# Trailing the second half of each output block by one more step, and spreading the second batch's filter products wider

## The chip, the cores and the metric

The kernel runs on one core of a Trainium2 chip. The metric is device time in microseconds (us) for one launch, and the time given for a kernel is the median of its runs. All profile times are us from the start of the profiled span, unless they are marked ns.

## The reference, cut to what matters

```python
# x: 8 batches x 3008 positions x 256 channels
X = np.fft.rfft(x, axis=1)
Y = X * (filt_r + 1j * filt_i)[None]          # one complex filter per frequency and channel
y = np.fft.irfft(Y, n=3008, axis=1)           # 24064 tokens x 256
h = y.reshape(24064, 256) @ w_in              # 256 -> 2048
g = h * sigmoid(beta * h)
out = g @ w_out                               # 2048 -> 256, float32
```

So there are two stages: a filter along the sequence, done batch by batch, and a two-layer network over all tokens.

## The kernel before

**The network.** The 24064 tokens are cut into 47 blocks of 512, and the hidden width of 2048 into 16 slices of 128. One *step* is one slice of one block, so there are 752 steps, and step s belongs to block s // 16. In a step TensorE makes the hidden slice `hps` (two matmuls of 512 columns), ScalarE applies the activation and writes `gT`, and some steps later TensorE takes `gT` as weights and adds the slice's part to the output sums `acc` (four matmuls of 256 columns, numbered tb 0 to 3, one for each 128 tokens of the block). Sums tb 0 and 1 share one PSUM bank (half 0 of a block), tb 2 and 3 another (half 1). The pool `opsum` has three banks and hands them out in turn: block i half 0, block i half 1, block i+1 half 0, and then block i+1 half 1 gets the bank of block i half 0 again. VectorE copies a finished bank to the SBUF tile `ost` (pool of two), and SyncE's queue stores `ost` to DRAM.

**The lag.** `lags[i]` says for each tb how many steps after its hidden slice the output matmul is issued. It is 2 for all four, except in the last block (2, 2, 4, 6). `gT` has seven buffers.

**The filter.** The Fourier transform of 3008 = 47 x 64 positions is done in four matmul stages, and for batches 1 to 7 these are strewn between the steps of the network: a dictionary `plan` lists, for each step, the helper calls that are issued after the step's hidden matmuls and before its output matmuls. In order, for a batch b:

- `load_x` (POOL's queue) brings x; `s1` (16 calls) makes the first transform into `a1`; `a2_load` turns `a1` by eight transposing DMAs in SyncE's queue.
- `s2` (12 calls) is the second transform and the filter product. TensorE makes two matmuls of 256 columns into a bank; VectorE makes three products of 512 elements a partition (`a_t`, and `b_t` in two halves); GpSimd adds them to `yh`.
- `s3` (12 calls, each a fixed number of steps after its `s2`) is the first inverse transform: two matmuls, and a copy into `z`. For batch 1 that copy is on ScalarE. After every third `s3` a DMA in SyncE's queue stores `z` to the scratch `d2`.
- `zz_load` brings `d2` back in four pieces (one for each two values of `jq`), again in SyncE's queue; the first waits until all of `d2` has landed.
- `s4` (16 calls) is the last transform. It writes `y`, which the network reads.

Batch 0 is done ahead of the steps, apart from the `f_late` and `z_late` calls in steps 1 to 26. `s1`, `s2`, `s3`, `s4` and `f_late` all draw from one pool of three PSUM banks, `fpsum`.

**Order.** The program is written in the order in which each engine runs it (a manual schedule). An engine works through its own list, and waits at an instruction until what it needs is there. So a call's step sets its place in every list: TensorE's, VectorE's, ScalarE's, GpSimd's and the queues of DMAs. A queue with nothing to wait for runs ahead of the step.

The main loop, for one step s: hidden matmuls, activation, the calls of `plan[s]`, then the output matmuls listed for s. With equal lags this list holds the four matmuls of slice s-2; after the last slice of a block both halves are copied out one after the other:

```python
    for h in range(2):
        evac(ost[:, 2 * h : 2 * h + 2, :], acc[i, h][:], False)
```

For batch 1 the filter products stand at steps 23 to 46, each `s3` five steps later (28 to 51), `zz_load` at step 54, `s4` at steps 66 to 78; the `s1` calls of batch 2 stand at steps 54 to 76, and the loads of batch 3's x at 62, 68, 88 and 92.

Of the kernel before, what the change touches and what calls it, by code (L numbers as in the profile page):

```python
# [10 lines left out]
P = 128  # L11
# [4 lines left out]
F32 = mybir.dt.float32  # L16
# [20 lines left out]
def kernel(  # L37
# [12 lines left out]
    B, S, D = x.shape  # L50
# [11 lines left out]
    NBLK = TOK // TB  # L62
# [43 lines left out]
    st = {}  # L106

    def evac(dst, src, on_act, scale=None):
        if on_act:
            nc.scalar.activation(dst, src, ACT.Copy, scale=1.0 if scale is None else scale)  # L110
        elif scale is None:
            nc.vector.tensor_copy(dst, src)  # L112
        else:
            nc.vector.tensor_scalar_mul(dst, src, scale)  # L114
# [440 lines left out]
    ostp = ctx.enter_context(tc.tile_pool(name="ostp", bufs=2, **tw))  # L555
# [116 lines left out]
    def at(s, fn, *a):  # L672
        plan.setdefault(int(s), []).append((fn, a))

    def s1_steps(b, units_, steps, act, on_act=()):
        assert len(steps) == len(units_)
        for i, s in zip(units_, steps):
            at(s, s1, b, i, i in on_act)

    def s23_steps(b, steps, lag, act):  # L680
        assert len(steps) == NU
        for i, s in enumerate(steps):
            at(s, s2, b, i)
            at(s + lag, s3, b, i, i % act == act - 1 if act else False)

    def s4_steps(b, steps, act):
        assert len(steps) == J // 4 * NDC
        for i, s in enumerate(steps):
            at(s, s4, b, i, i % act == act - 1 if act else False)

    for b in range(1, B):
        o = first_step[b - 1]
        if b == 1:
            at(1, z_late, 1, 0)
            at(2, z_late, 1, 1)
            s1_steps(1, range(16), [5 + (2 * i + 1) // 3 for i in range(16)], False, (1, 4, 7, 10, 13))
            for i, r in enumerate((3, 4, 5, 6)):
                at(r, f_late, 1, i // 2, i % 2)
            for g in range(NG):
                at(o + 17, a2_load, 1, g)  # L700
            for hh, z0, f0 in ((2, (4, 4), (16, 18, 19, 20)), (3, (5, 5), (21, 22, 24, 26))):
                for e in range(NDC):
                    at(z0[e], z_late, hh, e)
                for i, r in enumerate(f0):
                    at(r, f_late, hh, i // 2, i % 2)
            s23_steps(1, [o + r for r in (23, 25, 27, 29, 31, 34, 36, 38, 40, 42, 44, 46)], 5, 1)
            for h in range(J // JG):
                at(o + 54, zz_load, 1, h)
            s4_steps(1, [o + 66 + (i * 12) // 15 for i in range(16)], 2)
            at(0, scale_wout, 2 * WG)  # L710
            at(0, load_wout, 3 * WG)
            at(1, scale_wout, 3 * WG)
            if B > 2:
                for g in range(4):
                    at(o + 24 + 3 * g, load_x, 2, g)
                late = (54, 55, 56, 57, 58, 59, 60, 61, 66, 67, 68, 70, 72, 73, 74, 76)
                s1_steps(2, range(16), [o + r for r in late], False)
                for g in range(NG):
                    at(o + 80, a2_load, 2, g)
                if B > 3:  # L720
                    for g in range(4):
                        at(o + (62, 68, 88, 92)[g], load_x, 3, g)
            continue
        base = [o + 16 * n + s for n in range(4) for s in (4, 8, 12)]
        if b == 2:
            base[:6] = [o + r for r in (8, 12, 19, 22, 26, 29)]
        s23_steps(b, base, 6, False)
        for h in range(J // JG):
            at(o + 70, zz_load, b, h)
        s4_steps(b, [o + 80 + (i * 13) // 15 for i in range(16)], False)  # L730
        if b + 1 < B:
            early = [o + 16 * n + s for n in range(4) for s in (7, 13)]
            late = [o + s for s in (66, 67, 69, 70, 72, 73, 75, 76)]
            s1_steps(b + 1, range(16), early + late, False)
            for g in range(NG):
                at(o + 82, a2_load, b + 1, g)
            if b + 2 < B:
                for g in range(4):
                    at(o + (30, 62, 88, 92)[g], load_x, b + 2, g)

    blk = {}
    acc = {}
    lags = {i: (2, 2, 2, 2) for i in range(NBLK)}
    lags[NBLK - 1] = (2, 2, 4, 6)
    outs = {}
    for s in range(NSTEP):
        i, fb = divmod(s, NFB)
# [3 lines left out]
    def acc_of(i, tb):  # L751
        h = tb if i == NBLK - 1 and tb == 3 else tb // 2
        if (i, h) not in acc:
            acc[i, h] = opsum.tile([P, 2, D], F32, name="acc", tag="acc")
        return acc[i, h]

    def out_block(i):
        ost = ostp.tile([P, 4, D], F32, name="ost", tag="ost")
        rows = out[i * TB : (i + 1) * TB, :].rearrange("(c p) d -> p c d", p=P)
        for h in range(2):  # L760
            evac(ost[:, 2 * h : 2 * h + 2, :], acc[i, h][:], False)
        if i < HB:
            for h in range(2):
                off = (i * JG + 4 * h) * D
                dst = AP(out.tensor, out.offset + off, [[J * D, M], [D, 4], [1, D]])
                nc.sync.dma_start(dst, ost[h * M : (h + 1) * M, :, :])
            return
        nc.sync.dma_start(rows, ost[:])

    def out_last(i, tb, ost):  # L770
        rows = out[i * TB : (i + 1) * TB, :].rearrange("(c p) d -> p c d", p=P)
        if tb == 1:
            evac(ost[:, :2, :], acc[i, 0][:], True)
            nc.sync.dma_start(rows[:, :2, :], ost[:, :2, :])
        elif tb > 1:
            evac(ost[:, tb, :], acc_of(i, tb)[:, tb % 2, :], False)
            (nc.scalar if tb == 2 else nc.sync).dma_start(rows[:, tb, :], ost[:, tb, :])

    for s in range(NSTEP + 4):
        if s < NSTEP:  # L780
            i, fb = divmod(s, NFB)
            t0 = i * TB
            hps = hpsum.tile([P, TB], F32, name="hps", tag="hps")
            pos = t0
            while pos < t0 + TB:
                b, n0 = divmod(pos, S)
                ln = min(S - n0, t0 + TB - pos)
                for dc in range(NDC):
                    nc.tensor.matmul(  # L789
                        hps[:, pos - t0 : pos - t0 + ln],  # L790
                        lhsT=win_sb[:, dc, fb * P : (fb + 1) * P],
                        rhs=ys[b][:, dc, n0 : n0 + ln],
                        start=(dc == 0),
                        stop=(dc == NDC - 1),
                    )
                pos += ln
            gT = gpool.tile([P, TB], BF16, name="gT", tag="gT")
            nc.scalar.activation(gT[:], hps[:], ACT.Silu, scale=beta_sb[:, fb : fb + 1])  # L798
            blk[s] = gT
        for fn, a in plan.get(s, ()):  # L800
            fn(*a)
        last = NBLK - 1
        if s == NSTEP - 1:
            ost = ostp.tile([P, 4, D], F32, name="ost", tag="ost")
        for i, fb, tb in outs.get(s, ()):
            lone = i == last and tb > 1
            nc.tensor.matmul(  # L807
                acc_of(i, tb)[:, tb % 2, :],
                lhsT=blk[i * NFB + fb][:, tb * P : (tb + 1) * P],
                rhs=wout_sb[:, fb, :],  # L810
                start=(fb == 0 and (tb % 2 == 0 or lone)),
                stop=(fb == NFB - 1),
                skip_group_check=True,
            )
            if fb == NFB - 1:
                if i == last:
                    out_last(i, tb, ost)
                elif tb == 3:
                    out_block(i)
# [1 line left out]
_INS = ['x', 'filt_r', 'filt_i', 'moe_w_in', 'moe_w_out', 'moe_beta']  # L821
_OUTS = [((24064, 256), 'float32')]
# [25 lines left out]
```

## Time and profile before

| what | value |
|---|---|
| median of 3 runs | 774.1 us (773.82 to 774.34) |
| the profiled execution, its own time | 773.73 us |
| its span | 772.0 us |
| granted TensorE clock | 0.999 |
| TensorE matmul busy | 757.2 us, 98% |
| TensorE weight load busy | 547.9 us, 71% |
| ScalarE busy | 552.2 us, 72% |
| VectorE busy | 431.6 us, 56% |
| GpSimd busy | 152.9 us, 20% |

The profile belongs to one execution, whose time is 1.7 us above its span and 0.4 us below the median of the runs. In the profile PE is the matmul half of TensorE and PEld its weight load, DVE is VectorE, ACT ScalarE, POOL GpSimd, and SPq or POOLq the queue of DMA issues of that engine. L807 is line 807, the output matmul; L789 the hidden matmul; L798 the activation; L591 `s2`; L605, L606 and L609 its products; L610 the sum; L623 `s3`; L630 the store to `d2`; L635 `zz_load`; L645 `s4`; L564 `s1`; L580 `a2_load`; L112 VectorE's copies; L171 the loads of x. A matmul's duration includes its way through the array, so consecutive durations overlap; the distance between two starts tells how long one holds the engine.

### The profile page before, as it was taken

Reading aid. Unit: us, or ns where it says so; the run is one execution under the profiler, and the core shown is the slowest. Engines: PE = TensorE matmul, PEld = TensorE weight load, DVE = VectorE, ACT = ScalarE, POOL = GpSimd, SP = SyncE. Lnnn points to the kernel's source line nnn. Section 1 sums busy time; section 2 is a strip of 40 time slices with the busy share of each in tenths; the row PEclk is TensorE's granted clock in tenths of the full one; section 3 lists DMA queues with packets and bytes.
Section 4 is the critical chain, followed back from the end, with each engine's and each line's share of the span. In section 5 each row is a group of like instructions: output and inputs, shape, how many; then the busy total and the mean of one; then the engine's idle time right before and its main releaser. Section 6 shows DMA issues by size and latency. Waiting matters only on the chain.

```text
span 772.0 us, 15747 instructions
## 1 busy us (share of the span) xinstructions
PE 757.2 (98%) x6255; PEld 547.9 (71%) x6351; DVE 431.6 (56%) x712; ACT 552.2 (72%) x813; POOL 152.9 (20%) x155
## 2 busy tenths in 40 slices
PE   8899999999999999999999999999999999999997
PEld 5676777777777777867778777776777766676665
DVE  8869654765556655666456664566745665321001
ACT  7777877776677766777667776677766777777776
POOL 7805301222012220122101322022200222000000
PEclk9999999999999999999999999999999999999999
DMA  9998476334813258141672317621146111500101
GB/s 197 238 174 167 118 165 116 73 107 96 195 39 100 65 128 173 35 110 49 160 142 70 76 49 184 129 64 48 49 130 138 49 49 49 157 28 29 56 28 54
DMA packets 108348, 78.78 MB, mean 102 GB/s; under 512 B 53916, under 2 KB 101276, under 8 KB 108276
## 3 DMA queue, kind: packets, MB, share of 16 engines
q1 hardware_dynamic: 101876, 64.24, 32.1%
q0 software_dynamic: 4192, 13.40, 10.2%
q8 instruction: 49, 0.80, 0.4%
q10 hardware_dynamic: 2208, 0.14, 0.2%
q14 instruction: 23, 0.19, 0.1%
HBM read 43.46 MB, written 35.65 MB: 102 GB/s over the span
## 4 chain that ended last, share of the span: by engine, by line
PE 93%; DVE 3%; ACT 2%; issue 1%; POOL 0%; DVEq 0%; POOLq 0%
PE acc L807 43%; PE hps L789 39%; PE ps L645 3%; PE ps L564 3%; PE ps L623 2%; PE ps L591 2%; DVE a_t L605 1%; DVE b_t L606 1%; DVE b_t L609 0%; DVE ost L112 0%; ACT y L110 0%; ACT aT L110 0%; ACT t L110 0%; DVE pq_t L430 0%; PE sps L444 0%
## 5 line engine op out<-in xcount | busy, mean ns | idle before, releaser
L798 ACT ACTIVATE gT<-hps,beta_sb 128x512 bf16<-128x512 f32 x752 | 516.4, 687 | 207.4 <-PE hps L789 180.2
L807 PE MATMUL acc<-wout_sb,gT 128*128 128x256 bf16 x3008 | 453.3, 272 | 2.4
L789 PE MATMUL hps<-y,win_sb 128*128 128x512 bf16 (+7 forms) x1634 | 427.6, 350 | 0.2
L807 PEld LDWEIGHTS <-gT 128*128 128x128 bf16 x3008 | 280.8, 98 | 101.9 <-issue 1.2
L610 POOL TENSOR_TENSOR yh<-a_t,b_t 128x512 bf16<-128x512 f32 x84 | 106.6, 1269 | 419.2 <-DVE b_t L609 418.4
L789 PEld LDWEIGHTS <-win_sb 128*128 128x128 bf16 x1728 | 164.7, 98 | 24.5 <-DVE y L114 0.3
L112 DVE COPY ost<-acc 128x512 f32<-128x512 f32 (+1 forms) x94 | 60.0, 680 | 139.7 <-PE acc L807 139.7
L114 DVE TENSOR_SCALAR y<-ps 128x376 bf16<-128x376 f32 (+2 forms) x128 | 63.3, 510 | 61.9 <-PE ps L645 59.1
L605 DVE TENSOR_TENSOR a_t<-ps,fr_sb 128x512 f32<-128x512 f32 x84 | 58.1, 692 | 68.1 <-PE ps L591 67.5
L112 DVE CAST a<-ps 128x384 bf16<-128x384 f32 x107 | 59.1, 557 | 58.3 <-PE ps L564 47.8
L606 DVE SCALAR_TENSOR_TENSOR b_t<-ps,fi_sb 64x512 f32<-64x512 f32 x84 | 58.2, 693 | 1.1
L609 DVE TENSOR_TENSOR b_t<-ps,fi_sb 64x512 f32<-64x512 f32 x84 | 57.4, 684 | 1.1
L112 DVE CAST z<-ps 128x512 bf16<-128x512 f32 x72 | 49.4, 686 | 1.9 <-PE ps L623 1.0
L645 PEld LDWEIGHTS <-zz 96*128 96x128 bf16 x448 | 29.7, 97 | 22.9
L564 PEld LDWEIGHTS <-xg 94*128 94x128 bf16 x448 | 30.4, 97 | 19.9
L564 PE MATMUL ps<-t,xg 94*128 94x96 bf16 x448 | 36.7, 205 | 0.8
L645 PE MATMUL ps<-t,zz 96*128 96x94 bf16 x448 | 34.7, 205 | 1.1
L591 PE MATMUL ps<-a,t 128*128 128x256 bf16 x168 | 32.1, 273 | 0.6 <-DVE b_t L609 0.3
L623 PE MATMUL ps<-yh,t 128*128 128x256 bf16 x168 | 32.1, 272 | 0.5 <-DVE b_t L609 0.2
L623 PEld LDWEIGHTS <-t 128*128 128x128 bf16 x168 | 16.1, 98 | 18.1 <-issue 1.5
L591 PEld LDWEIGHTS <-t 128*128 128x128 bf16 x168 | 16.0, 98 | 16.6 <-DVE b_t L609 0.5
L171 POOL DMA_DIRECT2D xg<-in_x_dram x24 | 12.5, 523 | 54.8 <-PE ps L564 54.8
(96 smaller groups left out, 172.3 us busy)
## 6 DMA issues: line engine op xcount, KB each, us to landing
out_dram<-ost SPq DMA_DIRECT2D x42, 512.0 KB, 3.0
d<-z SPq DMA_DIRECT2D x28, 384.0 KB, 3.7
zz<-d SPq DMA_DIRECT2D x28, 384.0 KB, 6.6
xg<-in_x_dram POOLq DMA_DIRECT2D x24, 384.0 KB, 5.6
out_dram<-ost SPq DMA_DIRECT2D x9, 256.0 KB, 4.2
ws<-in_moe_w_out_dram SPq DMA_DIRECT2D x4, 512.0 KB, 7.5
fr_sb<-in_filt_r_dram SPq DMA_DIRECT2D x12, 128.0 KB, 4.3
fi_sb<-in_filt_i_dram SPq DMA_DIRECT2D x12, 128.0 KB, 4.3
```

Of the source, the lines that this page charges most:

```text
L112: nc.vector.tensor_copy(dst, src)
L114: nc.vector.tensor_scalar_mul(dst, src, scale)
L564: nc.tensor.matmul(ps[:, m * KP : (m + 1) * KP], lhsT=xg[b, g][:NP, m0 + m, e * P : (e + 1) * P], rhs=t1[:], start=True, stop=True,)
L591: nc.tensor.matmul(ps[:, e, :], lhsT=t2[:, k0 + e, :], rhs=st["a2", b, g][:, kk + e, :], start=True, stop=True,)
L605: nc.vector.tensor_tensor(a_t[:], ps[:], fr_sb[:, ks, :], ALU.mult)
L606: nc.vector.scalar_tensor_tensor(b_t[:M], ps[M:], -1.0, fi_sb[M:, ks, :], ALU.mult, ALU.mult)
L610: nc.gpsimd.tensor_tensor(yh[:], a_t[:], b_t[:], ALU.add)
L623: nc.tensor.matmul(ps[:, e, :], lhsT=t3[:, 2 * i + e, :P], rhs=yh[:, e, :], start=True, stop=True)
L645: nc.tensor.matmul(ps[:, e, :NP], lhsT=zz[:KP, j0 % JG + e, dc * P : (dc + 1) * P], rhs=t4[:], start=True, stop=True,)
L789: nc.tensor.matmul(hps[:, pos - t0 : pos - t0 + ln], lhsT=win_sb[:, dc, fb * P : (fb + 1) * P], rhs=ys[b][:, dc, n0 : n0 + ln], start=(dc ...
L798: nc.scalar.activation(gT[:], hps[:], ACT.Silu, scale=beta_sb[:, fb : fb + 1])
L807: nc.tensor.matmul(acc_of(i, tb)[:, tb % 2, :], lhsT=blk[i * NFB + fb][:, tb * P : (tb + 1) * P], rhs=wout_sb[:, fb, :], start=(fb == 0 an ...
```

## The change

Three things are changed, and no instruction is added or taken away.

1. In all blocks but the last, the output matmuls tb 2 and 3 come three steps after their hidden slice, not two.
2. Each half of a block is copied out as soon as its own last matmul is issued, so half 1 is copied one step after half 0. The store to DRAM stays one per block (two in the first four blocks) and follows half 1.
3. In batch 1, the `s2` calls stand at steps 23 to 50 where they stood at 23 to 46, the `s3` calls with them (28 to 55), and `zz_load` at step 57 where it stood at 54.

```diff
-            s23_steps(1, [o + r for r in (23, 25, 27, 29, 31, 34, 36, 38, 40, 42, 44, 46)], 5, 1)
+            s23_steps(1, [o + r for r in (23, 25, 28, 30, 34, 36, 38, 41, 43, 45, 47, 50)], 5, 1)
             for h in range(J // JG):
-                at(o + 54, zz_load, 1, h)
+                at(o + 57, zz_load, 1, h)
...
-    lags = {i: (2, 2, 2, 2) for i in range(NBLK)}
+    lags = {i: (2, 2, 3, 3) for i in range(NBLK)}
     lags[NBLK - 1] = (2, 2, 4, 6)
...
-    def out_block(i):
-        ost = ostp.tile([P, 4, D], F32, name="ost", tag="ost")
+    def out_half(i, h):
+        if h == 0:
+            st["ost", i] = ostp.tile([P, 4, D], F32, name="ost", tag="ost")
+        ost = st["ost", i]
+        evac(ost[:, 2 * h : 2 * h + 2, :], acc[i, h][:], False)
+        if h == 0:
+            return
         rows = out[i * TB : (i + 1) * TB, :].rearrange("(c p) d -> p c d", p=P)
-        for h in range(2):
-            evac(ost[:, 2 * h : 2 * h + 2, :], acc[i, h][:], False)
...
-                elif tb == 3:
-                    out_block(i)
+                elif tb % 2:
+                    out_half(i, tb // 2)
```

## The prediction

> **What bounds it.** I read the engine shares first, then the stretches, then the waits, and at last the timeline at single waits.
>
> ```profile
> PE 757.2 (98%) x6255; PEld 547.9 (71%) x6351; DVE 431.6 (56%) x712; ACT 552.2 (72%) x813; POOL 152.9 (20%) x155
> ...
> 0.00:34.00 34.00, 28.61 (x320) 20.19 (x324) 29.73 (x55) 25.28 (x36) 27.78 (x41) 1.00 1.01 219
> 34.00:60.00 26.00, 25.77 (x262) 19.16 (x265) 16.54 (x41) 18.56 (x30) 4.67 (x3) 1.00 1.00 179
> 60.00:80.00 20.00, 19.36 (x142) 13.46 (x143) 19.43 (x32) 15.37 (x26) 12.08 (x12) 1.00 0.87 182
> 200.00:300.00 100.00, 99.32 (x831) 72.14 (x842) 61.27 (x100) 69.35 (x102) 17.18 (x16) 1.00 0.44 106
> ...
> L807 PE MATMUL acc<-wout_sb,gT 128*128 128x256 bf16 x3008 | 453.3, 272 | 2.4
> ```
>
> The columns of a stretch are its length, then busy time of PE, PEld, DVE, ACT, POOL. TensorE is the bound everywhere after 34 us; only from 60 to 80 is another engine as full (DVE, 19.43 of 20). So the end moves only by what TensorE stops waiting, and the page's 2.4 us idle before L807 is nearly all there is. Busy time doesn't show short waits, so I laid the starts of all matmuls after 34 us one behind another: a 512-column matmul holds the engine 216 ns, 256 columns 108 to 109, 94 columns 41. What goes beyond is a wait. Two places show what they are:
>
> ```profile
> 198.95 0.60 PE L807 MATMUL acc<-wout_sb,gT 128*128 128x256 bf16 x4
> 199.39 0.59 PE L789 MATMUL hps<-y,win_sb 128*128 128x512 bf16 x2
> 199.62 1.28 DVE L112 COPY ost<-acc 128x512 f32<-128x512 f32 x2
> 199.99 0.74 PE L807 MATMUL acc<-wout_sb,gT 128*128 128x256 bf16 x4
> 200.35 0.10 PEld L807 LDWEIGHTS <-gT 128*128 128x128 bf16 x1 [0.15 <-issue]
> 200.57 0.59 PE L789 MATMUL hps<-y,win_sb 128*128 128x512 bf16 x2
> ```
>
> ```profile
> 70.02 0.38 PE L623 MATMUL ps<-yh,t 128*128 128x256 bf16 x2
> 70.63 1.29 DVE L112 COPY ost<-acc 128x512 f32<-128x512 f32 x2
> 70.66 0.39 PE L591 MATMUL ps<-a,t 128*128 128x256 bf16 x2 [0.26 <-DVE b_t L609]
> 70.89 0.87 PE L807 MATMUL acc<-wout_sb,gT 128*128 128x256 bf16 x4
> 71.60 0.59 PE L789 MATMUL hps<-y,win_sb 128*128 128x512 bf16 x2
> ```
>
> At 198.95 the four output matmuls take 0.44 us to the next hidden one. At 199.99, one step into a new block, they take 0.58: tb 2 opens half 1, its bank is the last block's half 0, and that copy runs from 199.62 to 200.30. The same at 70.89: 0.71 for 0.44. At 70.66 `s2` waits 0.42 for a bank that DVE's products still hold.
>
> The waits by size: **A**, tb 2 at a block's start: 0.27 at 71.4, and nineteen more of 0.07 to 0.14 between 88 and 742, 1.83 together: 2.10. **B**, the filter stretch: 0.10 at 63.7, 0.42 at 70.7, 0.12 at 78.4: 0.64. **C**, 0.13 at 756.1: at the last block the lag jumps from 2 to 4 and 6, two steps run without tb 2 and 3, and ACT (0.69 a step) falls behind. Sum 2.87, the most that can be won.
>
> **What the Trainium skill says.** "TensorE: Matmul & The Clock Gate", on the difference between 56 and 53.3 ns, gives 215.7 ns for 512 warm columns back to back; the trace's 216 agrees. "Perfetto Trace Analysis", Optimization Strategy, says that the same gap repeating on the engine that should be saturated can mean too few buffers for the next tile; A is that, 20 times. "DMA: Bandwidth & Descriptors", Queues, rings and completion order, says that a DMA engine takes turns between rings and consumes one ring in order. Both bear on the `zz` loads below; that a load in POOL's queue slows one in SP's agrees with the landings shown there.
>
> **Part by part.** *Lag and halves.* Same matmuls, copies and DMAs. The next block's tb 2 now comes one step later, so behind half 0's last matmul lie a whole step (0.864) and the hidden matmuls of the next (0.43): 1.30 us, where it was 0.216 + 0.43 + 0.216 = 0.86 without filter work. The copy needs about 0.2 to start, 0.69 and about 0.1 to be seen: 1.0. So the wait of 0.14 becomes a slack of 0.3, or more where filter calls lie between. DVE was idle ahead of the copy in 40 of 46 blocks (its wait for `acc` on the page of waits: 139.7 us, 40 times), so it isn't late; at 199.62 it was behind a `y` copy, and 0.3 covers that too. Half 1's bank isn't wanted for 16 steps. All of A goes: 2.10. `gT` lives four steps, of seven buffers. In the last block one light step is left instead of two, so C goes: 0.13. The skipped pair (0.216) is made up there: no sum changes.
>
> The queues: the block's store moves one step back. In batches 2 to 6 it thereby falls behind the eight transposes of `a2_load` (step o+82; 1.2 to 1.3 us each in SP's queue, some 10 us) and behind a `d2` store. `ost` has two buffers and is wanted again after 28 us, so the late store costs nothing; if it landed 14 us late, DVE would hold at the copy. Transposes start some 5 us sooner, behind the `zz` loads in the same queue; their result is wanted 18 steps later. Behind half 1's copy on DVE are products (step 4 of the block, two steps away) and `s1` copies, 0.56 us: covered.
>
> *Wider products.* A set of three costs 0.692 + 0.693 + 0.683 and gaps: 2.12 us of DVE. Before, steps 23 to 46 give TensorE's 25.6 us (activations at 58.55 and 84.14) for 11 sets (23.3), two `y` pairs (1.2) and block 1's copies (1.4): 25.9, so DVE falls behind and B follows. Now steps 23 to 50 give 28.1 for these and one half-copy more: 26.6, slack 1.5. Walking DVE's queue step by step (a step 0.864, `s2` and `s3` 0.217 each), each bank comes free ahead of its reuse but one: the eighth set (step 41) wants a bank at 76.9 that the seventh frees at 77.0. B's 0.64 becomes about 0.2 (bounds 0 to 0.6): won 0.44. POOL's `yh` (1.27) ends at least 0.35 ahead of each `s3`, the x loads in its queue included.
>
> *The `zz` chain.* This is what is late next. `s3` number 12 moves from step 51 to 55.
>
> ```profile
> 90.41 0.36 SPq L630 DMA_DIRECT2D d<-z  x1
> 94.64 2.53 SPq L635 DMA_DIRECT2D zz<-d  x4
> ...
> DMA to landing us min/median/max: 3.6/9.4/11.9
> ...
> 95.53 0.53 POOL L171 DMA_DIRECT2D xg<-in_x_dram  x1 [7.28 <-PE ps L564]
> ...
> 103.58 0.50 PE L645 MATMUL ps<-t,zz 96*128 96x94 bf16 x8
> ```
>
> Now it ran at 88.95, its store was issued 1.46 later, the first `zz` load 4.2 after that; it landed after 3.6 (98.3), ahead of the x load of 95.53; the second, beside that load, took 8.8 (104.0). `s4` begins at 103.58: 5.3 to spare for the first. After: step 55's hidden matmuls end at 92.81 in this trace, less the deferred pair 0.216, `s3` 12 itself 0.217, the waits up to there 0.99, plus 0.2: 91.6. Store 93.05, landed 2.8 to 4.1 later (both seen for `d2` stores), first `zz` load at 96.5. The x load comes 1.0 earlier, 94.5, so it is now ahead. `s4` wants the piece at 103.58 - 0.22 - 0.99 + 0.2 = 102.6. Landing between 3.6 (100.1) and 8.8 (105.3); I take 6.4, since the x load has two us of start: 102.9, a wait of **0.3** (0 to 2.7). The other pieces are wanted 3.5 us or more apart and landed 2.3 apart.
>
> **Sum.** 2.10 + 0.13 + 0.44 - 0.3 = 2.4 us. Profiled execution: 773.73 - 2.4 = 771.3. The median of the runs is 0.4 above that execution, so 771.7.
>
> **Rivals.** *The `zz` load late (slower).* Mechanism and place as above: the first piece behind the x load in the same DMA engines. Net zero comes from a landing at 102.6 + 2.7 = 105.3, slower by 0.2% (1.55 us, about what a measurement of this kernel can tell from no change) from 106.8. If it took 11.9 like the worst of four, 108.4, `s4` would wait 5.8: +3.1, 777.2. For it: only 5.3 to spare, 4 steps taken away. Against: the worst one stood third behind others in its ring, this stands first. Chance 0.07; ending near zero, 773.5 to 775, another 0.09.
>
> *The change doesn't do what it says.* If A came from DVE being late and not from the short distance, half 0 would still be late: gain 0.3 to 1.0, 773.4. For it: a `y` copy is ahead at 199.62. Against: 40 of 46 copies found DVE idle. Chance 0.09.
>
> *The filter stretch keeps its waits*, DVE's sum being the same: 2.1 + 0.13 - 0.3, 772.2. Chance 0.15, still faster.
>
> **The numbers.** The likeliest case (0.6) spans 771.2 to 772.6 and with the last rival gives 0.75 faster; the change without effect and the `zz` landing near zero give 0.18 within 0.2%; 0.07 slower. Leaving out the slow tail and little else: 771.0 to 774.0.
>
> **What would show it.** Right: idle before L807 falls from 2.4 to under 0.6; output matmuls of a block's first steps take 0.44 to the next hidden one; the copies stand singly, 0.68; 60 to 80 has PE above 19.7 busy; the first `s4` starts at 102.6 to 103. Wrong: idle before L645 or a first `s4` after 104; waits at L591 moved rather than gone; a new wait of `ost` for its store.

## The result and the profile after

The changed kernel takes 771.49 us (median of 6 runs, 770.99 to 772.39), the kernel before 774.16 beside it: a ratio of 0.9967, 95% interval 0.9954 to 0.998. That is 2.7 us, and the forecast was 2.4. The profiled execution took 771.2 us, with a span of 769.4 us where it was 772.0.

The shares of the engines on the page, three stretches of the table of stretches, and the row of the output matmul, which is now on line 810 (the hidden matmul is on 792):

```profile
PE 755.3 (98%) x6255; PEld 548.3 (71%) x6351; DVE 433.2 (56%) x712; ACT 552.3 (72%) x813; POOL 152.5 (20%) x155
...
60.00:80.00 20.00, 19.84 (x148) 14.21 (x149) 18.10 (x30) 16.03 (x26) 10.87 (x12) 1.00 0.85 175
80.00:120.00 40.00, 39.68 (x370) 29.17 (x375) 23.50 (x40) 31.17 (x52) 7.87 (x8) 1.00 0.59 137
200.00:300.00 100.00, 99.31 (x835) 72.56 (x845) 61.12 (x100) 69.68 (x102) 17.17 (x16) 1.00 0.55 110
...
L810 PE MATMUL acc<-wout_sb,gT 128*128 128x256 bf16 x3008 | 451.4, 272 | 2.3
```

From 60 to 80 TensorE is at 19.84 of 20 where it had 19.36, and VectorE has fallen from 19.43 to 18.10. In the stretch from 200 to 300 nothing seems to have happened: 99.31 was 99.32. The gain there shows only when the starts of the matmuls are laid one behind another. Of the waits over 0.05 us that the prediction listed after 34 us (2.87 us) none is left; the largest are 0.04 at an `s3` and 0.02 in the last block. (A gap of 0.18 ahead of a transpose of batch 0, at 34.3 before and 34.6 after, is in both and left out.) The last matmul starts at 765.30 and did so at 767.74, 2.44 earlier; the difference to 2.87 is mostly the part ahead of the steps, where the first hidden matmul came at 33.51 and before at 33.19, with the same code.

The same place as the one shown at 198.95 of the kernel before, in the timeline of the changed one:

```profile
197.94 0.60 PE L810 MATMUL acc<-wout_sb,gT 128*128 128x256 bf16 x4
198.38 0.59 PE L792 MATMUL hps<-y,win_sb 128*128 128x512 bf16 x2
198.61 0.68 DVE L112 COPY ost<-acc 128x512 f32<-128x512 f32 x1
198.98 0.60 PE L810 MATMUL acc<-wout_sb,gT 128*128 128x256 bf16 x4
199.42 0.59 PE L792 MATMUL hps<-y,win_sb 128*128 128x512 bf16 x2
199.66 0.68 DVE L112 COPY ost<-acc 128x512 f32<-128x512 f32 x1
```

The two copies stand singly, a step apart. The four output matmuls at 198.98 take 0.44 us to the next hidden one, where the ones at 199.99 took 0.58: half 0 is still being copied (198.61 to 199.29), but these matmuls don't want its bank yet.

And the chain that the prediction called next in line: the queue of SyncE, GpSimd's load of x, the landings of the first `zz` piece, and the first `s4`:

```profile
93.19 0.37 SPq L630 DMA_DIRECT2D d<-z  x1
96.18 2.25 SPq L635 DMA_DIRECT2D zz<-d  x4
...
94.67 0.53 POOL L171 DMA_DIRECT2D xg<-in_x_dram  x1 [3.87 <-PE ps L564]
...
DMA to landing us min/median/max: 6.0/6.0/6.0
...
102.72 0.50 PE L645 MATMUL ps<-t,zz 96*128 96x94 bf16 x8
```

The first piece landed at 96.18 + 6.0 = 102.2, and `s4` began at 102.72 without a wait. Before the change 5.3 us lay between these two; now 0.5.

### The profile page after: what moved, and what is told of

Its sections match the earlier page's. It is cut to its first block, busy times and chain, and to the rows that moved or that the text cites. A ratio compares the mean times of both kernels' runs of the same rounds, so it can differ in the third digit from the quotient of the medians.

```text
span 769.4 us, 15753 instructions
## 1 busy us (share of the span) xinstructions
PE 755.3 (98%) x6255; PEld 548.3 (71%) x6351; DVE 433.2 (56%) x712; ACT 552.3 (72%) x813; POOL 152.5 (20%) x155
## 4 chain that ended last, share of the span: by engine, by line
PE 94%; DVE 1%; DMA 1%; issue 1%; POOL 0%; SPq 0%; ACT 0%; DVEq 0%; POOLq 0%
PE acc L810 44%; PE hps L792 40%; PE ps L645 3%; PE ps L564 3%; PE ps L623 3%; PE ps L591 3%; DMA fi_sb<-in_filt_i_dram 1%; SPq L91 0%; PE ps L398 0%; DVE u L226 0%; DVE ost L112 0%; DVE pq_t L430 0%; DVE u L145 0%; DVE pq_t L427 0%; DVE y L114 0%
## 5 line engine op out<-in xcount | busy, mean ns | idle before, releaser
L810 PE MATMUL acc<-wout_sb,gT 128*128 128x256 bf16 x3008 | 451.4, 272 | 2.3
L112 DVE COPY ost<-acc 128x512 f32<-128x512 f32 (+1 forms) x94 | 63.5, 682 | 146.9 <-PE acc L810 146.8
```

The costliest lines, as they stand in the source:

```text
L810: nc.tensor.matmul(acc_of(i, tb)[:, tb % 2, :], lhsT=blk[i * NFB + fb][:, tb * P : (tb + 1) * P], rhs=wout_sb[:, fb, :], start=(fb == 0 an ...
```

## The experiments

In all of them the waits are read from the starts of the matmuls after 34 us of the profiled execution, as in the prediction.

**The wider products alone** (`spread_only`): the kernel before with this edit.

```diff
-            s23_steps(1, [o + r for r in (23, 25, 27, 29, 31, 34, 36, 38, 40, 42, 44, 46)], 5, 1)
+            s23_steps(1, [o + r for r in (23, 25, 28, 30, 34, 36, 38, 41, 43, 45, 47, 50)], 5, 1)
-                at(o + 54, zz_load, 1, h)
+                at(o + 57, zz_load, 1, h)
```

> Only the wider filter products of batch 1 (and zz_load at step 57); lags and copies as before. Theory (two separate causes): the waits B of the filter stretch go (0.64 us), the waits A at a block's start stay (2.1, of which the 0.27 at 71.4 may shrink to 0.14 because no product is queued ahead of the copy): idle that goes is 0.6 to 0.8 us, median 773.4 to 773.6. Rival (one cause, DVE too full in that stretch, makes both): most of the 2.7 goes, 771.5 to 772. Rival (the spreading does nothing): 774.1.

It took 773.11 us (772.64 to 774.56) beside 774.06, ratio 0.9989 (0.9982 to 0.9995). The waits of the filter stretch are gone, and so is the one at 71.4; 1.76 us of waits at blocks' starts remain. That is two causes, as the first theory has it. The medians differ by 0.95 us (interval 0.4 to 1.4), a little more than the 0.5 to 0.7 expected. In the profiled execution `s4` waits for a `zz` piece:

```profile
97.70 2.20 SPq L635 DMA_DIRECT2D zz<-d  x4
...
106.93 0.34 PE L645 MATMUL ps<-t,zz 96*128 96x94 bf16 x4 [0.28 <-DMA zz<-d]
```

It is not the first piece, which landed at 101.7, 1.0 ahead of the `s4` at 102.69. It is the second: it landed at 106.89, 8.6 us after its issue, and the `s4` at 106.93 is 0.44 late, read from the starts. So the margin of the `zz` chain was not enough here, at a piece for which the prediction allowed no wait. An `s3` at 132.7 waits 0.26 as well.

**The later half alone** (`lag_and_halves`): the changed kernel with the old steps for `s2` and `zz_load`.

> Only the later half 1 and the copies one by one; batch 1's products stay at steps 23 to 46. Theory: A goes (2.1), C goes (0.13), B stays at 0.3 to 0.6, since DVE's sum over these steps is as before less one half-copy: median 771.9 to 772.3. In the trace no wait at a block's start, one of 0.2 to 0.4 us at s2. Rival (DVE too full makes both): 773.5.

It took 772.52 us (771.88 to 773.26), ratio 0.9979 (0.9971 to 0.9987). No wait at a block's start is left in the profile. The time lies a little above the expected range (771.9 to 772.3), and so do the waits of the filter stretch: 0.98 us where 0.3 to 0.6 was expected and 0.64 stood before. They are in three places: 0.57 at two `s3`, and 0.42 at the same `s2` as before (the one shown):

```profile
69.89 0.38 PE L623 MATMUL ps<-yh,t 128*128 128x256 bf16 x2
70.53 0.39 PE L591 MATMUL ps<-a,t 128*128 128x256 bf16 x2 [0.26 <-DVE b_t L609]
70.76 0.60 PE L810 MATMUL acc<-wout_sb,gT 128*128 128x256 bf16 x4
71.19 0.59 PE L792 MATMUL hps<-y,win_sb 128*128 128x512 bf16 x2
```

From 69.89 two matmuls of 256 columns hold TensorE 0.22; the next starts 0.64 later. The output matmuls at 70.76 then go through in 0.43, where they took 0.71 before. Within their intervals the two gains add up: 0.95 and 1.54 us alone, 2.7 together.

**The lag without the split** (`lag_only`): the kernel before with one edit, so that both copies are still issued after tb 3.

```diff
-    lags = {i: (2, 2, 2, 2) for i in range(NBLK)}
+    lags = {i: (2, 2, 3, 3) for i in range(NBLK)}
```

> Only the lag of tb 2 and 3 (3 steps); both copies are still issued together after tb 3, so half 0's copy now stands on DVE behind the filter copies of one more step. Theory (the place on DVE's list decides): three blocks of each batch from 2 on have a filter copy in that step (z, z with a, y); half 0 is then done 2.1 to 2.9 us after its last matmul, while tb 2 of the next block wants it after 1.5 to 1.9: waits of 0.5, 0.8 and 1.0, about 2.3 us a batch, 13 in all, less the 1.3 of A that goes elsewhere: slower than before, 780 to 788. Rival (the copy waits for its bank alone, so the split is cosmetic and the lag does all): A goes, B stays, 772.

It took 794.67 us (793.09 to 795.93), ratio 1.0265 (1.0251 to 1.0279): slower by 20.6 us, and by 22 us than `lag_and_halves`, from which only the missing split sets it apart. So the split is not cosmetic. In the timeline of this kernel, in the third step of a block:

```profile
268.57 0.38 PE L623 MATMUL ps<-yh,t 128*128 128x256 bf16 x2
268.79 0.60 PE L807 MATMUL acc<-wout_sb,gT 128*128 128x256 bf16 x4
268.99 0.69 DVE L112 CAST z<-ps 128x512 bf16<-128x512 f32 x1 [2.47 <-PE ps L623]
269.60 1.28 DVE L112 COPY ost<-acc 128x512 f32<-128x512 f32 x2
270.33 0.33 PEld L807 LDWEIGHTS <-gT 128*128 128x128 bf16 x4 [1.01 <-DVE ost L112]
270.33 0.61 PE L807 MATMUL acc<-wout_sb,gT 128*128 128x256 bf16 x4 [0.52 <-DVE ost L112]
```

VectorE sat idle for 2.47 us ahead of the `z` copy, and half 0 was complete some 0.6 us before that ended (its last matmul starts at 268.03, fourth of the four at 267.70). But its copy stands behind the `z` copy on the list, and the `z` copy waits for an `s3` that TensorE reaches only at 268.57. Half 0 is copied at 269.60, and tb 2 of the new block, now the first output matmul of its step, waits for it. The waits come to 0.37 to 0.80 us in nearly every block of batches 2 to 7, with 2.28 in a block of batch 1: 21.2 in all in the profiled execution (793.09). My size was too small, since I had counted three such blocks a batch. There are five in most: a `z` copy stands in the third step of four of them, and `y` copies in that of a fifth. A split at a lag of 2 was not run: it gives the same order of instructions on every engine as the kernel before.

**All four trailing by three** (`lag3_all`): the changed kernel with lags (3, 3, 3, 3).

> As the changed kernel, but all four output matmuls trail by 3 steps, so both halves end in the same step. Theory (what counts is the distance between half 0's last matmul and the next half 1's first): it is 0.86 us again as before, A comes back with 1.8 to 2.1, B and C stay gone: 773.3 to 773.7. Rival (what counts is that gT is used later, and ACT has more room): as the changed kernel, 771.5.

It took 788.34 us (788.32 to 788.99), ratio 1.0186 (1.0172 to 1.02): neither theory. The waits at a block's start are back, but with 16.8 us they are eight times as large as before, most of them 0.46. The picture is close to that of the run above:

```profile
268.79 0.69 DVE L112 CAST z<-ps 128x512 bf16<-128x512 f32 x1 [2.47 <-PE ps L623]
269.39 1.28 DVE L112 COPY ost<-acc 128x512 f32<-128x512 f32 x2
269.45 0.38 PE L810 MATMUL acc<-wout_sb,gT 128*128 128x256 bf16 x2
270.13 0.38 PE L810 MATMUL acc<-wout_sb,gT 128*128 128x256 bf16 x2 [0.29 <-DVE ost L112]
```

Half 0's copy stands behind the `z` copy, and its bank is wanted at 269.67, 0.46 before it is free. The distance alone doesn't explain it. With a lag of 3 for all, half 0 ends in the third step of a block, where the filter copies stand; with a lag of 2 it ends in the second, where there are few. Two more runs tell this from a lag that is bad in itself.

**Lag 3 for all, with the filter copy moved away** (`lag3_s3_earlier`): as the last, and in batches 2 to 7

```diff
-        s23_steps(b, base, 6, False)
+        s23_steps(b, base, 5, False)
```

> Lag 3 for all four output matmuls, and s3 five steps after s2 in batches 2 to 7 (it was six), so that no z copy shares a step with half 0's copy. Theory (in the run with 3 for all, each wait is the short distance plus the z copy queued ahead on DVE): the waits of 0.46 fall to 0.08 to 0.15 as before the change; the two of 1.8 and 2.1 in batch 1 stay: 778 to 780. Rival (a lag of 3 is bad in itself): 788 as there.

It took 781.04 us (780.4 to 782.63), ratio 1.0095 (1.0079 to 1.011), 7.3 us less than without the edit. The waits at a block's start from batch 3 on are 0.07 to 0.15, the size they had before the change; the two in batch 1, where three products stand ahead of half 0's copy, are unchanged at 1.84 and 2.06. So the waits of 0.46 came from the `z` copy in the same step, not from the lag. The lag of 3 is not shown to be free, though: small waits stand at forty blocks' starts, 3.8 us together, where the kernel before had nineteen (1.83). The time is above the range expected, which left out these further waits, one of 0.46 in batch 2 (an `s3` stands in a block's third step there), a 0.75 us wait that the earlier `s3` brings at 136, and 0.5 us at two `s1`.

**Lags (3, 3, 4, 4)** (`lag3344`): half 1 trails by one step again, with half 0 in the crowded step.

> The changed kernel with lags (3, 3, 4, 4) in place of (2, 2, 3, 3): half 1 still trails by one step, and everything is one step later, so that half 0's copy falls in the step in which a z copy stands ahead of it on DVE. Theory (the distance of one step between the halves is what pays, and it covers a z copy): no wait at a block's start from batch 2 on; only blocks 1 and 2, where three products (2.1 us) stand ahead of the copy, keep 0.8 to 1.0 each: 772.8 to 773.5. Rival (the lag of 3 itself, or the step in which the copy falls, made the waits of the run with 3 for all): waits of 0.46 in most blocks as there, 785 or more.

It took 773.66 us (773.04 to 774.54), ratio 0.9994 (0.9986 to 1.0002). From batch 2 on no wait at a block's start is left; blocks 1 and 2 keep 0.97 and 1.19, and an `s1` at 38.5 waits 0.41, which puts the time just above the range of the first theory and far from the rival's 785. The third step of a block, where the run with 3 for all waited 0.46:

```profile
263.83 0.69 DVE L112 CAST z<-ps 128x512 bf16<-128x512 f32 x1 [2.47 <-PE ps L623]
264.06 0.59 PE L792 MATMUL hps<-y,win_sb 128*128 128x512 bf16 x2
264.44 1.28 DVE L112 COPY ost<-acc 128x512 f32<-128x512 f32 x2
264.50 0.60 PE L810 MATMUL acc<-wout_sb,gT 128*128 128x256 bf16 x4
264.93 0.59 PE L792 MATMUL hps<-y,win_sb 128*128 128x512 bf16 x2
```

Half 0's copy starts as late as there, behind the `z` copy, but the matmuls at 264.50 go through in 0.43. The step between the halves covers a `z` copy (0.69), and not three products (2.1).

**A fourth bank for the output sums** (`four_banks`): the kernel before with `opsum` at 4 and `fpsum` at 2.

> The kernel before with four banks for the output sums and two for the filter stages. Theory (A is a lack of a fourth bank): no wait at a block's start, gain 2.1; but two banks make the filter stages wait for their copies: s2 sets of 2.1 us on DVE then hold TensorE, and s1 and s4 beside each other as well; slower in all, 776 or more. Rival (A is DVE being late whatever the banks): waits at a block's start stay.

It took 792.79 us (792.56 to 793.37), ratio 1.0238 (1.0224 to 1.0251). No wait at a block's start is left: A was for want of a bank. But the filter stages with two banks wait 21.7 us. The two largest among TensorE's waits of this kernel (us in total, times, longest):

```profile
PE ps L623 <- DVE b_t L609: 8.6, 19, 0.8
PE ps L591 <- DVE b_t L609: 2.9, 8, 0.5
```

The bank is worth 2 us to one side and 20 to the other; a step of lag costs no bank.

**The changed kernel once more** (`after_again`).

> The changed kernel once more, beside the others: 771.0 to 772.0. In its trace no wait of TensorE over 0.05 us after 34 us, whichever execution is profiled; the stretch ahead of 34 us varies by some 0.3 us from one execution to the next.

It took 771.19 us (770.92 to 771.97), ratio 0.9959 (0.9946 to 0.9972). Its profile has one wait over 0.05 us, 0.16 at an `s3`, so "none" was not quite right. The first hidden matmul came at 33.36; over all the profiles here it lies between 33.19 and 33.56. The first `zz` piece landed 6.2 us after its issue at 96.02, 0.35 us ahead of the `s4` at 102.57.

**The last `s3` of batch 1 three steps later** (`last_s3_later`), to see whether the `zz` chain is next in line.

```diff
-            at(s + lag, s3, b, i, i % act == act - 1 if act else False)
+            late3 = 3 if b == 1 and i == NU - 1 else 0
+            at(s + lag + late3, s3, b, i, i % act == act - 1 if act else False)
...
-                at(o + 57, zz_load, 1, h)
+                at(o + 60, zz_load, 1, h)
```

> The changed kernel, with the last s3 of batch 1 at step 58 in place of 55, and zz_load at 60. In the changed kernel the first zz piece landed at 102.22, 0.5 us ahead of the s4 that reads it. Theory (this chain was next in line): the d2 store comes 3.1 us later, the first piece lands 6 to 7.5 us after its issue at 99.3, s4 of step 66 waits 2.6 to 4: 774 to 775.5, the gain lost. Rival (the piece came late only because of the x load ahead of it, and lands sooner when that is through): after 3.6 us, a wait of 0.2 to 0.5, 771.7 to 772.0.

It took 777.08 us (774.72 to 778.66, 12 runs), ratio 1.0032 (1.0023 to 1.0041). SyncE's queue and the first `s4` in the timeline:

```profile
96.30 0.37 SPq L630 DMA_DIRECT2D d<-z  x1
100.23 1.81 SPq L635 DMA_DIRECT2D zz<-d  x4
...
106.16 0.51 PE L645 MATMUL ps<-t,zz 96*128 96x94 bf16 x8 [3.29 <-DMA zz<-d]
```

The store took 3.9 us to land, the piece 5.9, and `s4` came 3.46 us late, within what the first theory said. The median lies above its range of 774 to 775.5, though: the runs spread over 4 us, and the profiled execution (774.72) is the fastest of them. The other eleven show a granted TensorE clock of 0.995 to 0.998, the profiled one 1.0. As an estimate, 0.002 to 0.005 of 775 us are 1.6 to 3.9 us, about the size of the spread. What lowered the clock, and whether the waits of these runs were longer too, was not seen.

**The same without the x loads beside it** (`later_no_x`): `load_x` of batch 3's first two pieces is replaced by a fill with zeros, so this kernel leaves those inputs out.

```diff
-                        at(o + (62, 68, 88, 92)[g], load_x, 3, g)
+                        at(o + (62, 68, 88, 92)[g], blank_x if g < 2 else load_x, 3, g)
...
+    def blank_x(b, g):
+        t = xpool.tile([KP, JG, D], BF16, name="xg", tag="xg")
+        nc.gpsimd.memset(t[:], 0.0)
+        xg[b, g] = t
```

> The changed kernel with the last s3 of batch 1 at step 58 and zz_load at 60 as in the earlier run, and with the first two x loads of batch 3 (which go beside the zz loads) replaced by a fill of the tile on GpSimd: those inputs are left out. Theory (the x loads on the same DMA engines stretch the d2 store and the zz piece): first zz piece lands 3.6 us after its issue instead of 5.9, d2 store after 2.8 instead of 3.9: the wait at s4 falls from 3.5 to 0.2 to 1.0, 771.6 to 772.5. Rival (the four pieces share among themselves): wait stays over 2.5, 774 or more.

It took 772.02 us (771.61 to 772.39), ratio 0.9971 (0.9961 to 0.9981). In the timeline, and in the landings of the first piece:

```profile
96.24 0.37 SPq L635 DMA_DIRECT2D d<-z  x1
99.13 2.00 SPq L640 DMA_DIRECT2D zz<-d  x4
...
DMA to landing us min/median/max: 4.0/4.0/4.0
...
103.15 0.51 PE L650 MATMUL ps<-t,zz 96*128 96x94 bf16 x8 [0.35 <-DVE ost L112]
```

The store at the same time is followed by the `zz` loads after 2.9 us where it was 3.9, the piece lands after 4.0 where it was 5.9, and `s4` starts 3.0 us earlier. So the x loads made up most of the wait. The runs no longer spread, and all show a clock of 0.999 or 1.0; of the 5.1 us between the two medians 3.1 are in the profiled executions. The part of the store is the less sure one: in `spread_only` it took 4.4 us and in the changed kernel 2.8, with the x load issued 1.5 us behind it in both. (The bracket puts what is left of the wait down to a copy that had long ended; the piece landed at 103.1.)

## Why the prediction was right, point by point

- **What bounds it.** Right: TensorE's waits were all there was to win, and nearly all of them went. The list by the starts of matmuls (2.87 us) held. That the end moved by 2.44 us, so near the 2.4 of the sum, is in part luck: the waits fell by 2.8, since the two terms named below at **B** and the `zz` chain cost nothing, and the first hidden matmul came 0.32 later.
- **A sign that failed.** I wrote that the 2.4 us idle on the page's row of L807 were nearly all there was, and that they would fall under 0.6. They are 2.3 after, with the waits gone. A matmul's row lasts 272 ns of which it holds TensorE for 108, so a wait up to some 0.16 us lies under the row before it and isn't idle time. It is counted as busy: the row's busy time fell by 1.9 us (453.3 to 451.4), and PE's by 1.9. That 2.4 came near the sum of A was chance.
- **A, the lag and the halves.** Right in size: 2.10 us went. The argument was incomplete. It rested on the distance from half 0's last matmul to the next half 1's first, and named a `y` copy as the worst ahead of half 0's. `lag3_all`, where distance alone predicted 773.5 and the chip gave 788.3, shows the other half: the copy must not stand behind a filter copy that waits for TensorE in the same step. With a lag of 2 and the copy split it doesn't.
- **C, the last block.** Right: 0.13 became 0.02.
- **B, the wider products.** Mis-sized: I left 0.2 for the eighth set's bank and nothing was left. The matmul ran at 77.22, while the seventh set's products ended only at 77.39, so it had another bank than in my walk through `fpsum`.
- **The `zz` chain.** The store was issued at 93.19 (93.05 forecast), the first `zz` load at 96.18 (96.5), the x load at 94.67 (94.5), and the piece took 6.0 us where I took 6.4. It was wanted at 102.72 (102.6), and was there 0.5 us early. The 0.3 us of wait didn't come in either profile of this kernel. The prediction took the later pieces to be safe, as they had landed 2.3 us apart; from the first to the second it had been 5.7, and in `spread_only` it was 5.2, where the second piece was 0.44 late.
- **The store behind the transposes.** As said, no wait for it is seen after.
- **The rivals.** The slower one, a late `zz` piece, has its mechanism shown: three steps more make the kernel slower than before, and taking the x loads away brings most of it back, though with a later `s3` than the changed kernel has. "The change doesn't do what it says" falls. "The filter stretch keeps its waits" falls for the changed kernel, and is what happens without the wider steps (`lag_and_halves`).

## What to carry to other kernels

When a bank is handed on in turn, its next user should come later than its last copy can end, and the copy should stand on its engine's list right behind the matmul that completes the bank: an engine in order lets a finished half lie behind a copy whose matmul has not run. Moving half the work by one step buys this without a buffer, where a further bank had to be taken from stages that needed it more. Look for short repeated waits in the distance between starts, not in idle time; and after spreading work wider, see how much room the transfer at its end has left.

## What the runs showed of the hardware

A load of x in GpSimd's queue can stretch a load of the same size in SyncE's queue, and it matters when it is issued. The first `zz` piece of 384 KB landed after 5.9 to 6.2 us in three profiles with an x load issued 1.4 or 1.5 us ahead of it. It landed after 3.6 with the x load 0.9 us behind, after 4.0 with one 3.1 us ahead and another 1.1 behind, and after 4.0 with none. Each of these is one execution.

The copies of the same time, 0.69 us each, cost 22 us more in one order than in another on one engine's list: with lags (2, 2, 3, 3) and the old filter steps the kernel took 772.52 us with the halves copied one by one and 794.67 with both copied after tb 3.
